# Seven products in place of eight for pairs of feature blocks in the first of two feed-forward stages

## The chip, the cores and the metric

One Trainium2 chip, one core of it. The metric is the device time in microseconds (us) of one execution of the whole program. The engines are TensorE (PE; the loads of its weights are shown as PEld), VectorE (DVE), ScalarE (ACT) and GpSimd (POOL); SyncE (SP) issues the loads.

## The reference

```python
def _moe_ref(x, w_gate, w_val, w_out):        # first stage, d_ff = 1536
    g = x @ w_gate
    silu = g * (1.0 / (1.0 + np.exp(-g)))
    val = x @ w_val
    return (silu * val @ w_out)

def _moe2_ref(x, w_in, w_out, alpha):         # second stage, d_ff = 2048
    h = x @ w_in
    g = np.maximum(h, 0.0) + alpha * np.minimum(h, 0.0)
    return (g @ w_out)

attn_out = _attn_ref(q, k, v, n_sink, window) # 2 batches, 8 heads, 768 positions, head size 64
x = attn_out.transpose(0, 2, 1, 3).reshape(1536, 512)
x = _moe_ref(x, w_gate, w_val, w_out)
return _moe2_ref(x, w_in, w_out, alpha)
```

The weights come as float64, 512 KB for 128 features. The result has the accuracy of float32.

## The kernel before

**The work.** 1536 tokens go through as three token blocks b = 0, 1, 2 of T = 512. Features are cut into blocks of 128: 12 in the first stage, 16 in the second. Every operand of a matmul is a pair of halves (h and l, type fp32r) whose sum is the float32 value, and a product of 128 rows of depth takes three matmuls of 512 columns: wh·xh, wh·xl and wl·xh. A block's projection (`proj`, L662) has four such rows of depth, so 12 matmuls.

**The weights.** `Stream` (L501) loads and converts them in the order of a list. SP loads a raw block (`raw`, three buffers); ACT takes its high words (Abs, L548, into `w_m`, two buffers); DVE puts the bits together (L584, L587, L590); ACT rounds to `wh` (L593); the rest `wl` is a subtraction (L599) on POOL if `idle_pool` is set, else on DVE. `step()` (L602) issues one stage of this after each piece of a unit. `idle_pool` is set during the attention and in the second stage. The `w_p` pool has 12 buffers for finished weights; chunk 1 of the first stage has 7 more (L1066).

**First stage.** `Moe1.unit(c, b)` (L688) takes a chunk c of four feature blocks and a token block b: gate projections `pg` (ACT makes `sg` with Silu, L710), value projections `pv` (DVE multiplies to `hid`, L718), the split of `hid` into `hh` (ACT, L679) and `hl` (DVE, L680), and four output products `po` of 12 matmuls each, which are copied (c = 0) or added by DVE (L742) to `acc`. 144 matmuls a unit, three chunks by three token blocks.

**Second stage.** `Duo.unit(c)` (L890) takes two feature blocks and all token blocks. Token blocks 0 and 1, the two feature blocks and the two halves of the depth form a 2 x 2 by 2 x 2 block product, which from c = 1 on is made with seven products of 6 matmuls (`product`, L835) and not eight. That needs sums of weights (kinds 2 and 3 in the list: POOL, L566 to L569, their `wh` by ACT, L572) and of tokens (`sums`, L819, 128x1024 operations taken one by one from the list `later`). Partial results stay in PSUM tiles `pa` and `pb`; ACT keeps copies of `pa` on the way (`keep`, L848, tiles p and u), which DVE adds to others (L855). Token block 2 goes through `proj`.

**Order.** The instructions' order on each engine is set by the framework's list scheduler from the order of the code; in the attention DVE's is as written. `verdict` (L362) makes a flag of range tests when the last weight is converted: one transpose `ps_flag` on PE, in the last but one unit of the second stage.

Of the kernel before, what the change touches and what calls it, by code (L numbers as in the profile page):

```python
# [35 lines left out]
WB = 12  # L36
WX = 7
RB = 3
VB = 6
# [20 lines left out]
def setup(nc, tc, ctx, g):  # L60
    const = ctx.enter_context(tc.tile_pool(name="const", bufs=1))
    g.const = const
    g.ident = const.tile([P, P], F32, name="ident")
    for nm in ("alpha", "sig", "sal", "sdn"):
        setattr(g, nm, const.tile([P, NF2], F32, name=nm))
    g.mask_a = const.tile([P, KW], F32, name="mask_a")
    g.mask_b = const.tile([P, KW], F32, name="mask_b")
    g.mask_0 = const.tile([P, P], F32, name="mask_0")
    g.mask_1 = const.tile([P, 2 * P], F32, name="mask_1")
    g.above = const.tile([P, P], I32, name="above")  # L70
    g.zero = const.tile([P, T], mybir.dt.bfloat16, name="zero")
# [83 lines left out]
def attention_pools(nc, tc, ctx, g):  # L155
    for nm, bufs in (("raw_p", VB), ("tr_p", TB), ("pr_p", 3), ("pt_p", 2), ("st_p", 4)):
        setattr(g, nm, ctx.enter_context(tc.tile_pool(name=nm, bufs=bufs)))
    g.nb = g.const.tile([P, B * H * NQ], F32, name="nb")
    g.wsum = g.const.tile([P, NW], F32, name="wsum")
    g.vsr = ctx.enter_context(tc.tile_pool(name="vs_p", bufs=1)).tile([P, NPAIR, NG * 2 * D], F32, name="vsr")  # L160
# [201 lines left out]
def verdict(nc, g):  # L362
    ok = g.const.tile([P, B * H * NQ], F32, name="ok")
    nc.vector.tensor_scalar(out=ok, in0=g.nb, scalar1=9.0e8, scalar2=None, op0=ALU.is_lt)
    red = g.red
    okw = g.const.tile([P, NW], F32, name="okw")
# [102 lines left out]
def weight_pools(nc, tc, ctx, g, sfx):  # L469
# [31 lines left out]
class Stream:  # L501
# [49 lines left out]
    def bits(self):  # L551
# [9 lines left out]
        if kind > 1:  # L561
# [10 lines left out]
            nc.scalar.activation(wh, m, AF.Copy)  # L572
# [5 lines left out]
        if slot is None or g.exact:  # L578
            nc.vector.tensor_scalar(out=m, in0=m, scalar1=WMAX, scalar2=-WMAX, op0=ALU.min, op1=ALU.max)
            w2 = g.w2_p.tile([P, KD * P], F32, tag="w2", name="w_2")  # L580
            sign, wi = mi, w2.bitcast(I32)
# [49 lines left out]
def moe1_seq(wg, wv, wo):  # L631
    seq = []
    for c in range(NF1 // CHUNK):
# [17 lines left out]
def duo_seq(wi, wo):  # L651

    seq = []
    for f in range(0, NF2, DUO):
        fs = range(f, f + DUO)
        seq += [(0, wi, x, DOWN, 3 * NF1 + x) for x in fs]
        seq += [(2, None, 0, None, None), (3, None, 0, None, None)] if f else []
        seq += [(1, wo, x, DOWN, 3 * NF1 + NF2 + x) for x in fs]
# [152 lines left out]
class Duo:  # L811
# [3 lines left out]
    def __init__(self, nc, g, st, base, ys, out, halves):  # L815
        self.nc, self.g, self.st, self.base, self.ys, self.out, self.halves = nc, g, st, base, ys, out, halves
        self.accs = {}

    def sums(self, a0, a1):  # L819

        nc, g = self.nc, self.g
        a, b, c, d = a0[:, 0:2], a0[:, 2:4], a1[:, 0:2], a1[:, 2:4]
        t1, t2, t4 = ([half(g.x_p2, n + z) for z in "hl"] for n in ("t1", "t2", "t4"))
        self.ts = ts = [t1, t2, [y[0] for y in self.ys[1]], t4]

        def sub(out, x, y):
            return lambda: nc.vector.tensor_tensor(out=out, in0=x, in1=y, op=ALU.subtract)

        def split(x, t):
            return lambda: split_hidden(nc, x, *t)  # L830

        self.last = split(c, ts[2])
        return [sub(a, c, a), sub(c, d, c), split(a, ts[0]), sub(d, d, a), split(d, ts[1]), sub(b, b, d), split(b, ts[3])]
# [19 lines left out]
    def add(self, ps, u):  # L853
        t = self.g.t_p.tile([P, T], F32, tag="hid", name="sum")
        self.nc.vector.tensor_tensor(out=t, in0=ps, in1=u, op=ALU.add)  # L855
        return t

    def bend(self, src, f, pair, inplace=False):
        nc, g = self.nc, self.g
        if inplace:  # L860
            hid = src
            nc.vector.scalar_tensor_tensor(
                out=hid, in0=src, scalar=g.alpha[:, f:f + 1], in1=src, op0=ALU.mult, op1=ALU.max
            )
        else:
            neg = g.t_p.tile([P, T], F32, tag="sg", name="neg")
            nc.scalar.activation(neg, src, AF.Copy, scale=g.alpha[:, f:f + 1])
            hid = g.t_p.tile([P, T], F32, tag="hid", name="hid2")
            nc.vector.tensor_tensor(out=hid, in0=src, in1=neg, op=ALU.max)
        split_hidden(nc, hid, *(t[:, f % 2] for t in pair))  # L870

    def plain(self):

        st, w, hids = self.st, self.base, {}
        for b, pool in ((0, None), (1, self.g.h_p2), (2, None)):
            hids[b] = hidden_pair(self.g, pool)
            for r in range(DUO):
                ph = self.new("ph")
                proj(self.nc, ph, st.get(w + r), *self.ys[b])
                self.bend(ph, r, hids[b])  # L880
                yield
            if b == 1:
                self.last()
        st.done(DUO)
        for b in range(3):
            for _ in self.outputs(0, b, w + DUO, *hids[b]):
                yield
        st.done(DUO)

    def unit(self, c):  # L890
        nc, g, st = self.nc, self.g, self.st
        if c == 0:
            yield from self.plain()
            return
        w = self.base + 2 * DUO + (c - 1) * 3 * DUO
        f = c * DUO
        (y0h, y0l), (y1h, y1l), y2 = self.ys
        b11, b21, b22 = (y0h[0], y0l[0]), (y0h[1], y0l[1]), (y1h[1], y1l[1])
        t1, t2, t3, t4 = self.ts
        hids = {0: hidden_pair(g)}  # L900
        pa, pb, pc = self.new("pa"), self.new("pb"), self.new("pc")
        self.product(pa, w, 0, b11, True)
        p1 = self.keep(pa, "p1")
        yield
        self.product(pc, w, 1, b21, True)
        self.bend(self.add(pc, p1), f, hids[0], True)
        yield
        self.product(pb, w + 2, 0, t1, True)
        yield
        self.product(pa, w + 2, 1, t2, False)  # L910
        u2 = self.keep(pa, "u2")
        yield
        hids[2] = hidden_pair(g)
        hids[1] = hidden_pair(g, g.h_p2)
        for r in range(DUO):
            ph = self.new("ph")
            proj(nc, ph, st.get(w + r), *y2)
            self.bend(ph, f + r, hids[2])
            yield
            if r == 0:  # L920
                self.product(pa, w + 3, 0, t3, False)
                u3 = self.keep(pa, "u3")
                self.bend(self.add(pb, u3), f + 1, hids[1], True)
                yield
        self.product(pa, w + 1, 1, t4, False)
        self.bend(pa, f + 1, hids[0])
        yield
        self.product(pb, w + 3, 1, b22, False)
        self.bend(self.add(pb, u2), f, hids[1], True)
        st.done(2 * DUO)  # L930
        yield
        for b in (2, 0, 1):
# [240 lines left out]
```

## Time and profile before

| | |
|---|---|
| three runs | 668.44, 670.21 (median), 671.40 us |
| the profiled execution, its own time | 670.04 us |
| its span, first to last instruction | 668.0 us |
| mean granted TensorE clock | 0.983 |
| busy: PE, DVE, ACT, POOL | 648.6, 430.7, 306.6, 158.6 us |
| first chunk's token block 2 starts | 181.09 us |
| 10 us windows with PE busy throughout at full clock | all from 180 to 660 us |

The span is what the trace shows; 2.0 us of the execution's own time lie outside it. PE is busy in 97% of the span, so what counts is how many matmuls there are, at which interval they follow each other, and where PE waits. Lines Lnnn are those of the kernel above. A matmul's own time (0.39 us) overlaps the next; the interval from one start to the next is what a matmul costs.

### The profile page before, as it was taken

The page shows a single profiled execution, that of the slowest core. Times are in us where ns is not written, and L with a number is a line of the kernel's source. Part 1 is how long each engine was busy: PE and PEld are TensorE (multiplying, and loading weights), DVE is VectorE, ACT ScalarE, POOL GpSimd, SP SyncE. Part 2 cuts the span into 40 slices and gives each one's busy share as a digit, 9 for nine tenths or more (in the row PEclk, how much of TensorE's full clock was granted, in tenths as well). Part 3 has the DMA queues.
Part 4 walks back from the last instruction along what each step waited for, and adds up shares of the span by engine and source line. Part 5 has one row for each costly group of instructions (what it writes and reads, how often), then busy time and mean ns, then how long its engine had stood idle before and what let it go on. Part 6 is the DMA issues. An engine that isn't in the chain of part 4 may idle for free.

```text
span 668.0 us, 8689 instructions
## 1 busy us (share of the span) xinstructions
PE 648.6 (97%) x3056; PEld 511.6 (77%) x3056; DVE 430.7 (64%) x915; ACT 306.6 (46%) x714; POOL 158.6 (24%) x203
## 2 busy tenths in 40 slices
PE   8879899999999999999999999999999999999996
PEld 4547566767788888888888888888888888888884
DVE  6897967355189852227432699938686969684654
ACT  4768755666366622024222356655344353533040
POOL 3547644334100000000000004614334251420000
PEclk8879899999999999999999999999999999999999
DMA  8754444100045620001300023222121303100005
GB/s 288 221 171 149 154 136 149 32 13 1 1 135 181 187 97 0 1 1 40 118 0 1 0 94 99 82 66 72 64 65 62 95 31 95 32 1 1 0 1 193
DMA packets 37203, 52.29 MB, mean 78 GB/s; under 512 B 4384, under 2 KB 28960, under 8 KB 37152
## 3 DMA queue, kind: packets, MB, share of 16 engines
q1 hardware_dynamic: 34944, 51.65, 24.2%
q8 instruction: 26, 0.43, 0.3%
q10 hardware_dynamic: 2208, 0.01, 0.2%
q14 instruction: 25, 0.20, 0.1%
HBM read 48.51 MB, written 3.15 MB: 77 GB/s over the span
## 4 chain that ended last, share of the span: by engine, by line
PE 88%; DVE 5%; ACT 3%; issue 1%; DMA 1%; POOL 1%; ACTq 0%; POOLq 0%
PE pf L947 7%; PE pf L948 7%; PE pf L949 7%; PE pa L841 6%; PE po L735 5%; PE pg L666 5%; PE po L736 5%; PE po L737 5%; PE pv L666 5%; PE pg L667 5%; PE pg L668 5%; PE pv L668 5%; PE pv L667 5%; PE pb L841 3%; PE ph L667 3%; PE ph L666 3%
## 5 line engine op out<-in xcount | busy, mean ns | idle before, releaser
L599 POOL TENSOR_TENSOR wl<-w_m,wh 128x512 fp32r<-128x512 f32 x44 | 57.9, 1322 | 99.1 <-ACT wh L593 87.1
L593 ACT ACTIVATE wh<-w_m 128x512 fp32r<-128x512 f32 x68 | 42.6, 629 | 76.9 <-PE pf L949 45.4
L947 PE MATMUL pf<-wh,hh 128*128 128x512 f32 x192 | 74.7, 389 | 0.0
L948 PE MATMUL pf<-wl,hh 128*128 128x512 f32 x192 | 74.7, 389 | 0.0
L679 ACT ACTIVATE hh<-hid 128x512 fp32r<-128x512 f32 x63 | 39.9, 633 | 66.7 <-DVE hid L718 51.7
L566 POOL TENSOR_TENSOR w_raw<-w_m 128x256 f32<-128x256 f32 x7 | 5.9, 840 | 253.0 <-DVE w_m L590 226.9
L949 PE MATMUL pf<-wh,hl 128*128 128x512 f32 x192 | 62.0, 389 | 0.0
L954 DVE TENSOR_TENSOR acc<-pf,acc 128x512 f32<-128x512 f32 x84 | 54.4, 681 | 11.4 <-PE pf L949 10.7
L718 DVE TENSOR_TENSOR hid<-pv,sg 128x512 f32<-128x512 f32 x36 | 24.7, 687 | 56.6 <-PE pv L668 56.5
L680 DVE TENSOR_TENSOR hl<-hid,hh 128x512 fp32r<-128x512 f32 x63 | 47.4, 754 | 20.7 <-ACT hh L679 20.3
L666 PE MATMUL pg<-xh,wh 128*128 128x512 f32 x144 | 57.5, 400 | 0.0
L666 PE MATMUL pv<-xh,wh 128*128 128x512 f32 x144 | 56.9, 395 | 0.0
L548 ACT ACTIVATE w_m<-w_raw 128x512 f32<-128x512 f32 x68 | 45.8, 674 | 24.0 <-DVE wl L599 9.6
L667 PE MATMUL pg<-xl,wh 128*128 128x512 f32 x144 | 56.7, 393 | 0.0
L668 PE MATMUL pg<-xh,wl 128*128 128x512 f32 x144 | 56.6, 393 | 0.0
L735 PE MATMUL po<-hh,wh 128*128 128x512 f32 x144 | 56.4, 395 | 0.0
L668 PE MATMUL pv<-xh,wl 128*128 128x512 f32 x144 | 56.1, 390 | 0.0
L667 PE MATMUL pv<-xl,wh 128*128 128x512 f32 x144 | 56.1, 389 | 0.0
L736 PE MATMUL po<-hh,wl 128*128 128x512 f32 x144 | 56.0, 390 | 0.0
L737 PE MATMUL po<-hl,wh 128*128 128x512 f32 x144 | 53.3, 390 | 0.0
L587 DVE SCALAR_TENSOR_TENSOR w_m<-w_raw,w_m 128x512 int32<-128x512 int32 x68 | 50.0, 736 | 1.1
L590 DVE SCALAR_TENSOR_TENSOR w_m<-w_raw,w_m 128x512 uint32<-128x512 uint32 x68 | 49.0, 723 | 0.6
(161 smaller groups left out, 1400.6 us busy)
## 6 DMA issues: line engine op xcount, KB each, us to landing
w_raw<-in_moe_w_out SPq DMA_DIRECT2D x28, 512.0 KB, 3.4
w_raw<-in_moe_w_in SPq DMA_DIRECT2D x16, 512.0 KB, 3.8
w_raw<-in_moe_w_gate SPq DMA_DIRECT2D x12, 512.0 KB, 4.4
w_raw<-in_moe_w_val SPq DMA_DIRECT2D x12, 512.0 KB, 4.4
th<-in_qk SPq DMA_DIRECT2D x16, 336.0 KB, 3.3
vr<-in_v SPq DMA_DIRECT2D x16, 192.0 KB, 2.6
out<-acc SPq DMA_DIRECT2D x12, 256.0 KB, 2.5
th<-in_qk SPq DMA_DIRECT2D x8, 256.0 KB, 5.1
```

The lines of the kernel that those rows point to most:

```text
L599: eng.tensor_tensor(out=wl, in0=m, in1=wh, op=ALU.subtract)
L666: nc.tensor.matmul(ps, wh[:, c], chan(xh, kk), start=(kk == 0), stop=False)
L667: nc.tensor.matmul(ps, wh[:, c], chan(xl, kk), start=False, stop=False)
L668: nc.tensor.matmul(ps, wl[:, c], chan(xh, kk), start=False, stop=(kk == KD - 1))
L735: nc.tensor.matmul(ps, wh[:, mc], hh, start=(x == 0), stop=False)
L736: nc.tensor.matmul(ps, wl[:, mc], hh, start=False, stop=False)
L737: nc.tensor.matmul(ps, wh[:, mc], hl, start=False, stop=(x == CHUNK - 1))
L841: self.nc.tensor.matmul(ps, a[:, c], m[:, k], start=(start and k == 0 and y == 0), stop=(k == 1 and y == 2), skip_group_check=True)
L947: nc.tensor.matmul(ps, hh[:, x, ts], wh, start=(x == 0), stop=False)
L948: nc.tensor.matmul(ps, hh[:, x, ts], wl, start=False, stop=False)
L949: nc.tensor.matmul(ps, hl[:, x, ts], wh, start=False, stop=(x == DUO - 1))
L954: nc.vector.tensor_tensor(out=av, in0=ps, in1=av, op=ALU.add)
```

## The change

Chunk 0 of the first stage stays. Its eight other feature blocks are taken by pairs by a new class `Duo1`: blocks 4, 5 plain; 6, 7 and 8, 9 with seven products for the gate and again for the value; 10, 11 plain, with the outputs. The code of the seven products becomes `Chain`, for both stages. The second stage keeps its steps.

```diff
-WB = 12
-WX = 7
+ORDER7 = (1, 2, 5, 6, 8, 7, 9, 4, 3)
+WB = 10
 RB = 3
+WA = 2
...
-            nc.scalar.activation(wh, m, AF.Copy)
+            nc.gpsimd.tensor_copy(wh, m)
             self.halves = (i, m, wh, wl)
...
+def duo1_seq(wg, wv, wo):
+
+    seq = []
+    for f in range(CHUNK, NF1, DUO):
+        fs = range(f, f + DUO)
+        more = SUMS if CHUNK < f < NF1 - DUO else []
+        seq += [(0, wg, x, DOWN, x) for x in fs] + more
+        seq += [(0, wv, x, DOWN, NF1 + x) for x in fs] + more
+        seq += [(1, wo, x, DOWN, 2 * NF1 + x) for x in fs]
+    return seq
...
+    def plus(self, ps, u, b, r):
+        t = self.room(b, r)
+        self.duo.nc.vector.tensor_tensor(out=t, in0=ps, in1=u, op=ALU.add)
+        self.sink(b, r, t, True)
+
+    def step(self, x):
+        d, w = self.duo, self.w
+        b11, b21, b22, t1, t2, t3, t4 = self.ops
+        if x == 1:
+            self.a = d.new("pa")
+            d.product(self.a, w, 0, b11, True)
+            self.p1 = d.keep(self.a, "u1")
+        elif x == 2:
+            ps = d.new("pc")
+            d.product(ps, w, 1, b21, True)
+            self.plus(ps, self.p1, 0, 0)
+        elif x == 6:
+            d.product(self.a, w + 2, 1, t2, False)
+            self.u2 = d.keep(self.a, "u2")
+        elif x == 5:
+            self.b = d.new("pb")
+            d.product(self.b, w + 2, 0, t1, True)
+        elif x == 7:
+            d.product(self.a, w + 3, 0, t3, False)
+            self.plus(self.b, d.keep(self.a, "u1"), 1, 1)
+        elif x == 4:
+            d.product(self.a, w + 1, 1, t4, False)
+            self.sink(0, 1, self.a, False)
+        elif x == 3:
+            d.product(self.b, w + 3, 1, b22, False)
+            self.plus(self.b, self.u2, 1, 0)
+        else:
+            ps = d.new("ph")
+            proj(d.nc, ps, d.st.get(w + x - 8), *self.more)
+            self.sink(2, x - 8, ps, False)
...
+        u, v = (g.h_p2.tile([P, 2, T], F32, tag=z, name="tsum") for z in ("hh", "hl"))
+        return [
+            self.sub(u, c[0], a[0]), self.add(u, u, c[1]), self.sub(u, u, a[1]),
+            self.sub(v, d[0], u), self.split(u, t1), self.add(v, v, d[1]),
+            self.sub(u, b[0], v), self.split(v, t2), self.add(u, u, b[1]),
+            self.sub(v, d[0], c[0]), self.split(u, t4), self.add(v, v, d[1]), self.sub(v, v, c[1]), lambda: self.third(v),
+        ]
...
+        def gate(b, r, src, own):
+            t = src if own else room_g(b, r)
+            nc.scalar.activation(t, src, AF.Silu)
+            gates[b, r] = t
...
+        def value(b, r, src, own):
+            hid = src if own else room_v(b, r)
+            nc.vector.tensor_tensor(out=hid, in0=src, in1=gates[b, r], op=ALU.mult)
+            split_hidden(nc, hid, *(t[:, r] for t in pairs[b]))
...
+        if c in (0, last):
+            yield from self.plain(w, c == last)
+            return
+        pairs = self.pairs()
+        room_g, gate, room_v, value = self.sinks(pairs)
+        for i, room, sink in ((0, room_g, gate), (2 * DUO, room_v, value)):
+            chain = self.chain(w + i, self.ops, self.xs[2], room, sink)
+            yield from chain.steps(ORDER7)
+            chain.done()
+        for b in (2, 0, 1):
+            for m in range(KD):
+                self.output(b, m, w + 4 * DUO, *pairs[b])
+                yield
+        self.st.done(DUO)
...
+        for x in range(DUO):
+            wh, wl = st.get(w + x)
+            nc.tensor.matmul(ps, wh[:, mc], hh[:, x], start=(x == 0), stop=False)
+            nc.tensor.matmul(ps, wl[:, mc], hh[:, x], start=False, stop=False)
+            nc.tensor.matmul(ps, wh[:, mc], hl[:, x], start=False, stop=(x == DUO - 1))
+        av = self.accs[b][0][:, m]
+        nc.vector.tensor_tensor(out=av, in0=ps, in1=av, op=ALU.add)
...
+    add_pool(nc, tc, early, g.w_ps, "w_pa", WA, "right")
+    st.own = range(3 * CHUNK)
...
+    for nm, bufs in (("x_p2", 6), ("u_p", 1), ("h_p2", 1), ("t_p2", 4)):
+        setattr(g, nm, ctx.enter_context(tc.tile_pool(name=nm, bufs=bufs)))
+    st.idle_pool = True
...
+    later.extend(d1.sums())
+    run([m1.unit(0, 2)])
+    assert g.w_ps.pop()[1] == WA
+    early.close()
+    last = (NF1 - CHUNK) // DUO - 1
     with ExitStack() as inner:
-        add_pool(nc, tc, inner, g.w_ps, "w_p2", WX)
-        run([m1.unit(0, 2)] + [m1.unit(1, b) for b in range(NPASS)])
-        assert g.w_ps.pop()[1] == WX
...
+        g.x_p3 = inner.enter_context(tc.tile_pool(name="x_p3", bufs=2, side="right"))
+        run([d1.unit(c) for c in range(last)])
+        assert not later
+    add_pool(nc, tc, ctx, g.w_ps, "w_p3", WA, "right")
+    st.own = range(base - 3 * DUO, len(st.seq))
+    run([d1.unit(last)] + [d2.unit(c, ys) for c in range(NF2 // DUO)])
```

The first change of code is that of the weight sums (kinds 2 and 3). Finished weights so have 12 buffers in chunk 0, 10 while the token sum t3 holds the place of two, and 12 from the last pair on. Masks and other constants of the attention move to a pool that ends with it, a temporary of the general path becomes the raw block's place, and `verdict` takes its scratch from the pool of `hid`.

The scheduler's order changes with it. PE, value products of blocks 8 and 9 (`pa`, `t2` to `t4` are the chain's partial result and token sums, `po` an output product of the same unit), as it is now:

```order
L1013 MATMUL po_3425<-hh_3082,wh_3097 128x512
L1014 MATMUL po_3425<-hh_3082,wl_3098 128x512
L846 MATMUL pa_3202<-t3h_2370,wh_3012 128x512
L846 MATMUL pa_3202<-t3l_2371,wh_3012 128x512
L846 MATMUL pa_3202<-t3h_2370,wl_3013 128x512
L846 MATMUL pa_3202<-t3h_2370,wh_3012 128x512
L846 MATMUL pa_3202<-t3l_2371,wh_3012 128x512
L846 MATMUL pa_3202<-t3h_2370,wl_3013 128x512
L1015 MATMUL po_3425<-hl_3083,wh_3097 128x512
L846 MATMUL pa_3202<-t4h_2049,wh_2979 128x512
```

Step 4 (t4) adds to `pa` one matmul after step 7 (t3), whose value ACT has to keep in between.

ACT, last pair of the first stage (blocks 10, 11), token block 2 (`w_m` are weights in conversion, `hh_3762` the upper half of the hidden pair that the outputs read, `yh` and `t1h`, `t2h` the second stage's tokens and token sums), as it is now:

```order
L953 ACTIVATE sg_3793<-ph_3780 128x512
L691 ACTIVATE yh_3713<-acc1_1899 128x512
L592 ACTIVATE wh_3847<-w_m_3826 128x512
L548 ACTIVATE w_m_3853,wsum_125<-w_raw_3573 128x512
L548 ACTIVATE w_m_3880,wsum_125<-w_raw_3599 128x512
L691 ACTIVATE hh_3762<-hid_3816 128x512
L691 ACTIVATE t2h_3758<-acc1_1899 128x1024
L691 ACTIVATE hh_3762<-hid_3841 128x512
```

The split of `hid_3816` stands behind a rounding and two steps of conversion; before, the outputs of a token block came from four hidden blocks and not from two.

PE, last but one unit of the second stage, before (`ps_flag` is the verdict's transpose, `pa`, `pb`, `pc` the chain's partial results, `t1` a token sum):

```order
L841 MATMUL pc_5376<-yl_3198,wh_4976 128x512
L841 MATMUL pc_5376<-yh_3196,wl_4977 128x512
L373 MATMUL ps_flag_5419<-ident_61,one_5417 1x128
L841 MATMUL pb_5375<-t1h_3463,wh_5012 128x512
L841 MATMUL pb_5375<-t1l_3464,wh_5012 128x512
```

and now:

```order
L846 MATMUL pa_5517<-t2l_3759,wh_5159 128x512
L846 MATMUL pa_5517<-t2h_3758,wl_5160 128x512
L846 MATMUL pa_5517<-yh_3712,wh_5175 128x512
L846 MATMUL pa_5517<-yl_3714,wh_5175 128x512
L846 MATMUL pa_5517<-yh_3712,wl_5176 128x512
L846 MATMUL pa_5517<-yh_3712,wh_5175 128x512
L846 MATMUL pa_5517<-yl_3714,wh_5175 128x512
L846 MATMUL pa_5517<-yh_3712,wl_5176 128x512
L373 MATMUL ps_flag_5560<-ident_61,one_5558 1x128
L846 MATMUL pb_5567<-t1h_3756,wh_5159 128x512
```

Steps 6 (t2) and 7 (y) now follow each other directly in `pa`, and the transpose and step 5 (t1) come behind them; before, step 5 stood ahead of step 6, and twelve matmuls of a projection lay between 6 and 7.

## Rows read from the trace of the kernel before

**Rows 1.** Page, part 1: busy time, share of the span, instructions.

```profile
PE 648.6 (97%) x3056; PEld 511.6 (77%) x3056; DVE 430.7 (64%) x915; ACT 306.6 (46%) x714; POOL 158.6 (24%) x203
```

**Rows 2.** Busy time by stretch; columns: stretch, then each engine, granted clock, DMA share, GB/s.

```profile
10.00:20.00 10.00, 8.83 (x43) 5.32 (x44) 8.51 (x36) 7.46 (x33) 5.01 (x6) 0.66 1.07 390
40.00:50.00 10.00, 8.70 (x41) 5.25 (x42) 8.81 (x44) 6.18 (x26) 4.37 (x6) 0.66 0.42 128
...
140.00:150.00 10.00, 9.16 (x54) 6.16 (x53) 5.01 (x21) 6.73 (x16) 2.21 (x5) 1.00 0.00 0
...
200.00:210.00 10.00, 10.00 (x45) 8.26 (x44) 9.74 (x19) 5.13 (x11) 0.00 (x0) 1.00 0.51 165
240.00:300.00 60.00, 60.00 (x267) 49.67 (x266) 14.62 (x23) 9.21 (x15) 0.00 (x0) 1.00 0.04 14
...
390.00:660.00 270.00, 270.00 (x1193) 223.50 (x1192) 198.42 (x313) 117.33 (x218) 75.82 (x66) 1.00 0.19 62
```

**Rows 3.** What PE waited for, whole span, largest and smallest: total, times, longest.

```profile
PE ps_s L224 <- ACT pr L234: 5.6, 8, 1.5
...
PE xp L320 <- POOL pt L295: 0.4, 1, 0.4
```

**Rows 4.** Timeline of PE, a pair of the second stage: start, length, instruction.

```profile
598.74 0.39 PE L841 MATMUL pa<-yh,wh 128*128 128x512 f32 x1
...
599.87 0.39 PE L841 MATMUL pa<-yh,wl 128*128 128x512 f32 x1
...
601.23 0.39 PE L841 MATMUL pc<-yh,wl 128*128 128x512 f32 x1
```

**Rows 5.** Timeline of ACT, the same place.

```profile
600.30 0.60 ACT L850 ACTIVATE p<-pa 128x512 f32<-128x512 f32 x1 [0.73 <-PE pa L841]
```

**Rows 6.** DVE by line and shape, 180 to 668: busy us, mean ns, idle before.

```profile
L599 DVE TENSOR_TENSOR wl<-w_m,wh 128x512 fp32r<-128x512 f32 x31 | 21.0, 685 | 2.1 <-ACT wh L593 1.9
L718 DVE TENSOR_TENSOR hid<-pv,sg 128x512 f32<-128x512 f32 x28 | 19.3, 688 | 49.5 <-PE pv L668 49.5
...
L742 DVE TENSOR_TENSOR acc<-po,acc 128x512 f32<-128x512 f32 x24 | 15.8, 686 | 24.1 <-PE po L737 23.8
...
L855 DVE TENSOR_TENSOR sum<-pb,u 128x512 f32<-128x512 f32 x14 | 9.6, 686 | 6.7 <-ACT u L850 6.7
...
L827 DVE TENSOR_TENSOR acc<-acc,acc 128x1024 f32<-128x1024 f32 x3 | 3.7, 1218 | 0.0
```

**Rows 7.** ACT by line and shape, 180 to 668.

```profile
L548 ACT ACTIVATE w_m<-w_raw 128x512 f32<-128x512 f32 x54 | 36.3, 673 | 21.4 <-DVE wl L599 9.6 <-POOL wl L599 6.1 <-POOL w_m L568 2.7
L593 ACT ACTIVATE wh<-w_m 128x512 fp32r<-128x512 f32 x56 | 35.0, 628 | 69.0 <-PE pf L949 45.4 <-PE pa L841 7.8 <-PE po L737 6.7
L679 ACT ACTIVATE hh<-hid 128x512 fp32r<-128x512 f32 x55 | 34.8, 632 | 60.3 <-DVE hid L718 45.3 <-DVE hid L869 15.0
...
L548 ACT ACTIVATION_READ_ACCUMULATOR w_m<-w_raw 128x1 f32 x54 | 10.3, 191 | 0.0
```

**Rows 8.** POOL by line and shape, 180 to 668.

```profile
L599 POOL TENSOR_TENSOR wl<-w_m,wh 128x512 fp32r<-128x512 f32 x32 | 42.6, 1339 | 77.0 <-ACT wh L593 64.9 <-PE pf L949 11.4
...
L568 POOL TENSOR_TENSOR w_m<-w_m 128x256 f32<-128x256 f32 x7 | 8.1, 1154 | 0.2
L567 POOL TENSOR_TENSOR w_raw<-w_raw,w_m 128x256 f32<-128x256 f32 x7 | 6.6, 938 | 0.1
L566 POOL TENSOR_TENSOR w_raw<-w_m 128x256 f32<-128x256 f32 x7 | 5.9, 840 | 253.0 <-DVE w_m L590 226.9 <-PE pa L841 26.1
L569 POOL TENSOR_TENSOR w_m<-w_m,w_raw 128x256 f32<-128x256 f32 x7 | 5.7, 808 | 0.0
```

**Rows 9.** Timeline of POOL, start of the second stage.

```profile
427.62 1.82 POOL L599 TENSOR_TENSOR wl<-w_raw,wh 128x512 fp32r<-128x512 f32 x1 [1.21 <-PE pf L949]
```

**Rows 10.** Timeline of DVE, the same place.

```profile
428.20 1.79 DVE L590 SCALAR_TENSOR_TENSOR w_m<-w_raw,w_m 128x512 uint32<-128x512 uint32 x1
```

More of the change, by code (lines that the diff above doesn't have):

```diff
@@ L628, in done, with moe1_seq @@
             self.n_done += 1
-def moe1_seq(wg, wv, wo):
+def moe1_seq(wg, wv, wo, chunks=NF1 // CHUNK):
     seq = []
-    for c in range(NF1 // CHUNK):
+    for c in range(chunks):
         fs = range(c * CHUNK, (c + 1) * CHUNK)
@@ L655, in duo_seq @@
         fs = range(f, f + DUO)
-        seq += [(0, wi, x, DOWN, 3 * NF1 + x) for x in fs]
-        seq += [(2, None, 0, None, None), (3, None, 0, None, None)] if f else []
+        seq += [(0, wi, x, DOWN, 3 * NF1 + x) for x in fs] + (SUMS if f else [])
         seq += [(1, wo, x, DOWN, 3 * NF1 + NF2 + x) for x in fs]
@@ L811, with __init__, sub, add @@
 class Duo:
[L815 to L833, printed above, removed]
+    def __init__(self, nc, g, st):
+        self.nc, self.g, self.st = nc, g, st
+    def sub(self, out, x, y):
+        return lambda: self.nc.vector.tensor_tensor(out=out, in0=x, in1=y, op=ALU.subtract)
+    def add(self, out, x, y):
+        return lambda: self.nc.vector.tensor_tensor(out=out, in0=x, in1=y, op=ALU.add)
+    def split(self, x, t):
+        return lambda: split_hidden(self.nc, x, *t)
     def product(self, ps, w, r, x, start):
@@ L872, in plain @@
[L872 to L932, printed above, removed]
-            for _ in self.outputs(c, b, w + 2 * DUO, *hids[b]):
-                yield
@@ new lines, in chain, with pairs, __init__, steps @@
+    def chain(self, w, ops, more, room, sink):
+        return Chain(self, w, ops, more, room, sink)
+    def pairs(self):
+        g = self.g
+        return {b: hidden_pair(g, pool) for b, pool in ((0, g.h_p), (2, g.h_p), (1, g.h_p2))}
+class Chain:
+    def __init__(self, duo, w, ops, more, room, sink):
+        self.duo, self.w, self.ops, self.more, self.room, self.sink = duo, w, ops, more, room, sink
+    def plus(self, ps, u, b, r):
[32 more added lines that the diff above has]
+            self.sink(2, x - 8, ps, False)
+    def steps(self, order):
+        for x in order:
+            self.step(x)
+            yield
+    def done(self):
+        self.duo.st.done(2 * DUO)
@@ L1063, in run @@
                     asked = True
-    with ExitStack() as inner:
-        add_pool(nc, tc, inner, g.w_ps, "w_p2", WX)
-        run([m1.unit(0, 2)] + [m1.unit(1, b) for b in range(NPASS)])
-        assert g.w_ps.pop()[1] == WX
-    for nm, bufs in (("x_p2", 6), ("u_p", 1), ("h_p2", 1)):
-        setattr(g, nm, ctx.enter_context(tc.tile_pool(name=nm, bufs=bufs)))
-    run([m1.unit(2, b) for b in range(NPASS)])
-    st.idle_pool = True
-    run([m2.unit(c) for c in range(NF2 // DUO)])
-    assert asked
+    later.extend(d1.sums())
+    run([m1.unit(0, 2)])
+    assert g.w_ps.pop()[1] == WA
+    early.close()
+    last = (NF1 - CHUNK) // DUO - 1
+    with ExitStack() as inner:
+        g.x_p3 = inner.enter_context(tc.tile_pool(name="x_p3", bufs=2, side="right"))
[4 more added lines that the diff above has]
+    run([d1.unit(last)] + [d2.unit(c, ys) for c in range(NF2 // DUO)])
+    assert asked and not later
 def general(nc, tc, g, q, k, v, w_gate, w_val, w_out, x2_in, x2_out, out):
```

171 lines of the change are left out of this document (132 added, 39 removed).

## The prediction

> **What bounds the kernel now.** I read the page first: PE is busy in 97% of the span, DVE in 64%, ACT in 46%, POOL in 24% [rows 1]. Then the busy time by stretch, because a share of the whole says nothing of a stage. From 390 to 660 us PE works for 270.00 of 270 us at full clock, and so it does in 240 to 300, where DVE has only 14.62 of 60 us of work [rows 2]. PE's waits come next: the list for the whole span begins with 5.6 us and ends with 0.4, and all of it is of the attention (ps_s, xp, ps_p) [rows 3]; from 170 us on it is empty. So behind the attention the time is the number of matmuls times their interval. The timeline of PE gives that interval: from 598.74 to 601.23 eleven of them, 0.2264 us each [rows 4]. The 0.39 us of a row is a matmul's own length and overlaps the next. A matmul taken out there is worth 0.226 us, one waited for costs the wait, and work on another engine costs nothing as long as PE finds its operands in time.
>
> **What is removed from PE.** A seven-product chain has 42 matmuls for token blocks 0 and 1 where eight products have 48. The change makes four such chains: gate and value, for blocks 6, 7 and for 8, 9. That is 4 x 6 = 24 matmuls, and 24 x 0.2264 = 5.43 us. The other matmuls (token block 2, outputs, both plain pairs) are as many as before. The attention keeps its order on PE up to the first chunk, and the second stage has the same steps, so I cost both at nothing, but for one place below.
>
> **What is added on the other engines, and why most of it costs nothing.** The outputs of a pair of blocks are six matmuls long and not twelve, so 48 additions come where DVE had 24 at 686 ns (L742): 16.5 us more. Twelve additions of kept partial results at 686 ns (L855) are 8.2 us. The token sums are ten operations and four splits of 128x1024 at 1218 ns (L827): 17.1 us. Off DVE go the `wl` subtractions, 31 at 685 ns: 21.2 us [rows 6]. Net 20.6 us on an engine that has 237 us free [rows 1]. By stretch the tightest is the first chunk's token block 2 with the sums, where DVE had 9.74 of 10 us already [rows 2], part of it those subtractions. I put it at up to 38 us of work in a unit of 33, but its late pieces (the sums) are needed only a unit later, and the plain pair between (216 matmuls, 49 us) takes up the rest. A seven-product unit has about 34 us of DVE work in 204 matmuls or 46 us. POOL gets 40 subtractions at 1339 ns, four weight sums of 840 + 938 + 1154 + 808 = 3740 ns [rows 8] and the 22 roundings of sums that ACT did or would do. A rounding on POOL is not in the trace; I bound it by ACT's 628 ns [rows 7] and POOL's 1339 for a subtraction, and take the latter, being POOL's own row of the same size: 29 us. Sum 98 us, on an engine that was idle from 180 to 390 us. The four extra weight pairs need no loads. The loads on SP's queue are as many as before; with 12 or 10 buffers in place of 19 they start later, but a weight is still finished 15 us or more before PE's order asks for it, by my count of the matmuls between. Constants that moved cost nothing for the same reason: they are in place when their readers start, as before.
>
> **Where PE now has to wait.** What a short chain costs is read at the second stage, where the same steps run. The last matmul of a `pa` product starts at 599.87 [rows 4], ACT begins to copy it at 600.30 and takes 0.60 [rows 5]. A matmul that writes to `pa` again can follow 0.43 + 0.60 = 1.03 us after that start, which is four and a half intervals. In three places of the new order the distance is smaller than the chain:
> 1. Blocks 8, 9, value: step 4 follows step 7 with one output matmul between, two intervals. 1.03 - 0.45 = 0.58 us. Nothing shortens it; it is longer, up to 1.4, if ACT is in a conversion step (673 + 191 ns [rows 7]) just then. I take 0.6.
> 2. Last pair, token block 2: `hh_3762` stands on ACT behind the rounding `wh_3847`, which waits for the weight buffer that PE gives back 14 matmuls ahead of the reader `po_3861`, and behind a conversion step that waits for POOL's subtraction from that rounding (two `w_m` buffers). Chain: 0.43 + 0.63 (rounding) + 1.34 (POOL [rows 8]) + 0.67 + 0.19 (conversion) + 0.63 (`hh`) [rows 7] = 3.89 us against 14 x 0.2264 = 3.17. I take 0.7; the bounds are 0 (the rounding finds its buffer earlier) and 1.4 (DVE is in a 1218 ns sum as `hid_3816` comes).
> 3. Last but one unit of the second stage: steps 6 and 7 are neighbours. 1.03 - 0.23 = 0.80 us; there were twelve matmuls between.
> 4. First plain pair, token block 0: `hh_2327` is behind the conversion of `w_m_2429`, which waits for the weight sums on POOL (two subtractions and L566 to L568, 2 x 1.34 + 2.93 = 5.6 us). By my count of what lies between it just fits or misses by 0.5; if POOL is late by half of that chain, 3 us. I take 0.3, near the end that the count gives.
>
> Everywhere else I find a margin: the least is 0.6 us, at the first split of the first seven-product unit, and the others are 1.2 or more.
>
> Rows that stretch two of these terms: a POOL subtraction beside a DVE operation took 1.82 us, and DVE's 1.79 where its mean row is 0.72 [rows 9, 10]. The Trainium skill ("GPSIMD Engine Reference", section 1, Specifications) says that POOL shares its SBUF interfaces with VectorE and that they contend when DVE has two SBUF inputs; these two rows agree, and by that rule place 2 would use 1.82 and not 1.34, which makes its term 1.2 and the sum 667.5. I stay with the mean over 32 of them, which has such meetings in it.
>
> **The sum.** The profiled execution took 670.04 us, 668.0 of it span; it is 0.17 below the median of the three runs, which is nothing beside their own spread of 3 us. 670.04 - 5.43 + 0.6 + 0.7 + 0.8 + 0.3 = **667.0 us**. Smallest terms (0.58, 0, 0.80, 0): 666.0. Largest (1.4, 1.4, 0.8, 3): 671.2. What a measurement of this kernel can tell from no change is about 0.5%, 3.4 us: below 666.86 is faster, above 673.56 slower. The forecast sits at that line: a real gain of which half is given back.
>
> **The rivals.**
> - *No wait remains.* The order is a list; engines run ahead where they can, and if the kept copies and splits come a little sooner than in my chains, all of 5.43 us stays: 664.6. For it: the second stage runs the same chain seven times with no wait of PE [rows 2]. Against it: places 1 and 3 are closer than any place there, and a copy of 0.60 us cannot be hidden behind one matmul.
> - *POOL holds up everything (slower).* With `wl`, the sums and their roundings on POOL and only two `w_m` buffers, the conversion step after each of the four new sum pairs waits for two subtractions and the sum, 2.68 + 3.74 = 6.4 us, and it stands on ACT and DVE ahead of the copies and splits that PE needs next. If the cover is the twelve matmuls of one projection (2.7 us), PE loses 3.7 us at each: 664.6 + 4 x 3.7 = 679.4. From 2.2 us each on it is slower by over 0.5% (8.9 us in all). For it: ACT's conversion steps already wait for POOL (6.1 and 2.7 us of their idle time [rows 7]), and meetings with DVE stretch POOL further [rows 9]. Against it: the same sum pairs in the second stage cost PE nothing in 270 us [rows 2], with the same two buffers.
> - *A wait takes the clock down.* In 10 to 20 and 40 to 50 us PE was busy for 8.83 and 8.70 of 10 us and the granted clock was 0.66; with 9.16 it stayed at 1.00 [rows 2]. The waits that I count leave 9.2 or more. If one of them is as long as there (1.2 us), the 10 us are worth 6.6: one such fall costs 3.4 us, and the time is 667.0 + 3.4 = 670.4, no change.
> - *DVE becomes the bound in the first chunk's last unit.* If PE does have to wait for DVE's 38 us in 33, 5 us: 672.0. It needs a sum ahead of a split that PE reads soon; in the order the sums stand behind them or a unit ahead.
>
> **How the numbers follow.** The forecast has 0.58, no wait at all 0.20, a fall of the clock or DVE as the bound together 0.10, POOL 0.12. Faster by over 0.5%: the second case, and nearly half of the first (666.0 to 666.86, where the unknown terms are at their low ends): 0.47. Slower: POOL's, 0.12. The rest, 0.41, lies within 0.5%. The range goes from 664.5 (no wait) to 671.0, which takes in the largest terms and the fall of the clock and leaves out POOL's case and half of DVE's. The likeliest case's own range is 666.0 to 669.
>
> **What the profile of the changed kernel would show.** PE: 24 matmuls fewer, interval 0.226, and a list of PE's waits behind 170 us that is no longer empty: three or four entries of 0.3 to 1 us, `pa` after the kept copies (L855) in two places and `po` after `hh`. If the list is empty, the first rival holds; if it has entries of 2 us and more for `hh` or `wl` behind POOL, the second. The granted clock should be 1.00 in every stretch from 180 us on. DVE should show about 450 us, POOL about 255. The forecast is wrong if the attention ends at another time than 181.09, for which I have no term, or if a fifth place appears.

## The result and the profile after

The changed kernel takes 674.14 us (median of six runs, 673.59 to 675.3) against 669.38 before; the ratio is 1.0069, interval 1.0052 to 1.0086. It is slower by 0.7%; I had forecast 667.0, and 664.5 to 671.0 as the range. The profiled execution took 675.3 us, its span is 673.6.

The page and the list of PE's waits from 170 us on, of the changed kernel (engine, line, waited for; total, times, longest):

```profile
PE 650.3 (97%) x3032; PEld 508.5 (75%) x3032; DVE 473.9 (70%) x933; ACT 308.5 (46%) x716; POOL 245.2 (36%) x281
```

```profile
PE po L1013 <- ACT hh L691: 4.5, 2, 2.5
PE pa L846 <- ACT u L855: 1.1, 2, 0.7
```

PE has the 24 matmuls fewer [rows 1]. The list, empty before, has two lines of two waits each, and these are the four places that I had named. DVE is busy for 473.9 us where I had forecast about 450, POOL for 245.2 and not 255. The waits as listed start where the last matmul's 0.39 us end; what a wait costs is the interval from start to start less the usual 0.2265. Worked out so from the starts of all matmuls, between the attention's last matmul and the last of all (the stretch, 480.14 us before and 484.12 now):

| term | forecast | measured, us |
|---|---|---|
| 24 matmuls fewer | -5.43 | -5.44 |
| place 1, step 4 behind step 7 | 0.6 | 0.62 |
| place 2, last pair, token block 2 | 0.7 | 2.70 |
| place 3, step 7 behind step 6 | 0.8 | 0.85 |
| place 4, first plain pair, token block 0 | 0.3 | 2.14 |
| first interval behind a wait, and one more of that size, 5 x 0.11 | none | 0.55 |
| matmuls that follow each other more slowly | none | 2.55 |
| sum | -3.0 | +3.97 |

The sum is the measured +3.98. In this execution the attention ends 2.02 us later too, one of the signs that the prediction named for its being wrong; 1.2 us of it come where the granted clock stays low for longer, 0.73 in 80 to 90 us against 0.88 before. The change does not make it so each time: two executions of the same order of instructions below (e2, e10) had their attention as short as before, 179.74 and 179.73 us from the first matmul against 179.81. So what there is to explain is two waits, and matmuls that got slower without any wait.

**Place 4.** POOL, ACT, DVE and PE of the changed kernel in the first plain pair (start, length, instruction; in brackets the idle time before):

```profile
220.94 1.83 POOL L598 TENSOR_TENSOR wl<-w_m,wh 128x512 fp32r<-128x512 f32 x1 [2.85 <-ACT wh L592]
222.72 0.75 POOL L566 TENSOR_TENSOR w_raw<-w_m 128x256 f32<-128x256 f32 x1
223.42 1.30 POOL L598 TENSOR_TENSOR wl<-w_m,wh 128x512 fp32r<-128x512 f32 x1
224.67 0.75 POOL L567 TENSOR_TENSOR w_raw<-w_raw,w_m 128x256 f32<-128x256 f32 x1
225.50 0.74 POOL L568 TENSOR_TENSOR w_m<-w_m 128x256 f32<-128x256 f32 x1
```

```profile
226.27 0.66 ACT L548 ACTIVATE w_m<-w_raw 128x512 f32<-128x512 f32 x1 [3.02 <-POOL w_m L568]
226.83 0.19 ACT L548 ACTIVATION_READ_ACCUMULATOR w_m<-w_raw 128x1 f32 x1
228.40 0.63 ACT L691 ACTIVATE hh<-hid 128x512 fp32r<-128x512 f32 x1 [1.38 <-DVE hid L961]
```

```profile
227.05 0.72 DVE L583 TENSOR_SCALAR w_m<-w_m 128x512 int32<-128x512 int32 x1 [5.44 <-ACT w_m L548]
227.69 0.68 DVE L961 TENSOR_TENSOR hid<-ph,sg 128x512 f32<-128x512 f32 x1
```

```profile
226.72 0.39 PE L680 MATMUL ph<-xh,wl 128*128 128x512 f32 x1
229.08 0.50 PE L1013 MATMUL po<-hh,wh 128*128 128x512 f32 x1 [1.98 <-ACT hh L691]
```

This is the chain that I had written down, POOL's sums and then the conversion step on ACT, with one link more: that step's first half on DVE, and only then `hid` and `hh`. DVE is idle for 5.44 us, though the last matmul of the product that `hid` reads had started 12 intervals ahead of 226.72; `hid` stood second in DVE's queue.

**Place 2.** DVE, POOL and ACT in the last pair of the first stage, changed kernel:

```profile
399.20 2.60 DVE L692 TENSOR_TENSOR yl<-acc,yh 128x512 fp32r<-128x512 f32 x2
401.72 1.21 DVE L692 TENSOR_TENSOR t1l<-acc,t1h 128x1024 fp32r<-128x1024 f32 x1
402.86 2.31 DVE L832 TENSOR_TENSOR acc<-acc 128x1024 f32<-128x1024 f32 x1
405.10 0.68 DVE L692 TENSOR_TENSOR yl<-acc,yh 128x512 fp32r<-128x512 f32 x1
405.70 0.68 DVE L961 TENSOR_TENSOR hid<-ph,sg 128x512 f32<-128x512 f32 x1
```

```profile
399.64 1.61 POOL L598 TENSOR_TENSOR wl<-w_m,wh 128x512 fp32r<-128x512 f32 x1
402.35 1.73 POOL L598 TENSOR_TENSOR wl<-w_m,wh 128x512 fp32r<-128x512 f32 x1 [1.10 <-ACT wh L592]
```

```profile
404.12 0.67 ACT L548 ACTIVATE w_m<-w_raw 128x512 f32<-128x512 f32 x1 [1.19 <-POOL wl L598]
...
406.41 0.63 ACT L691 ACTIVATE hh<-hid 128x512 fp32r<-128x512 f32 x1 [1.52 <-DVE hid L961]
```

PE at the same place, the last matmul of the product that this `hid` reads and the first one that waits for `hh`:

```profile
401.44 0.39 PE L680 MATMUL ph<-xh,wl 128*128 128x512 f32 x1
...
407.09 0.50 PE L1013 MATMUL po<-hh,wh 128*128 128x512 f32 x1 [2.54 <-ACT hh L691]
```

The matmuls between the two, up to 404.16, make the other block's product. My chain over POOL ends on ACT at 404.9; by itself it would have cost about 1.2 us (an estimate: `hh` from 404.9 with its 0.63, against PE's next turn at 404.39). But `hh` starts 1.5 us later, because `hid` is late. Its product is there from 401.8 on, and DVE first works off splits and token sums for almost 4 us: one of 128x1024 beside POOL's subtraction takes 2.31, the one ahead of it 1.21.

**The slow matmuls.** PE in the second stage of the changed kernel; the moving operand is a weight in one of the two lent buffers at the upper end of the memory:

```profile
441.60 0.40 PE L1098 MATMUL pf<-wh,hh 128*128 128x512 f32 x1
...
443.00 0.40 PE L1098 MATMUL pf<-wh,hh 128*128 128x512 f32 x1
```

Six intervals in 1.40 us, 0.2333 each, with no wait between. By the program's addresses it is the 312 matmuls whose moving operand lies in those two buffers (t3 first, then weights): 6.6 ns longer than 0.2265 on the mean, the others 0.4. In the kernel before, where all operands start at the same offset within 256 bytes, the mean is 0.2 ns over 0.2265. What such small differences come to, without waits and the intervals behind them, I call the small excess: 2.96 us here, 0.40 before. Nothing in my prediction had a term for that.

### The profile page after: what moved, and what is told of

It reads as the page before. It is cut to its first block, busy times and chain, and to the rows that moved or that the text cites. A ratio compares the mean times of both kernels' runs of the same rounds, so it can differ in the third digit from the quotient of the medians.

```text
span 673.6 us, 8796 instructions
## 1 busy us (share of the span) xinstructions
PE 650.3 (97%) x3032; PEld 508.5 (75%) x3032; DVE 473.9 (70%) x933; ACT 308.5 (46%) x716; POOL 245.2 (36%) x281
## 4 chain that ended last, share of the span: by engine, by line
PE 84%; DVE 7%; ACT 4%; POOL 2%; issue 1%; DMA 1%; SPq 0%; POOLq 0%; ACTq 0%
PE pa L846 9%; PE pf L1100 7%; PE pf L1099 7%; PE pf L1098 7%; PE ph L678 6%; PE ph L679 6%; PE ph L680 6%; PE pb L846 4%; PE po L1013 3%; PE po L1014 3%; PE po L1015 3%; PE ps_s L224 2%; PE xp L320 2%; PE pc L846 2%; PE po L747 2%; PE po L748 2%
## 5 line engine op out<-in xcount | busy, mean ns | idle before, releaser
L598 POOL TENSOR_TENSOR wl<-w_m,wh 128x512 fp32r<-128x512 f32 x79 | 111.6, 1419 | 197.8 <-ACT wh L592 172.9
L583 DVE TENSOR_SCALAR w_m<-w_m 128x512 int32<-128x512 int32 x68 | 34.5, 508 | 38.6 <-ACT w_m L548 38.6
L680 PE MATMUL ph<-xh,wl 128*128 128x512 f32 x128 | 49.8, 389 | 0.0
L679 PE MATMUL ph<-xl,wh 128*128 128x512 f32 x128 | 49.8, 389 | 0.0
L678 PE MATMUL ph<-xh,wh 128*128 128x512 f32 x128 | 49.8, 389 | 0.0
L234 ACT ACTIVATE pr<-ps_s,nb 128x160 f32<-128x160 f32 (+2 forms) x96 | 38.0, 406 | 19.0 <-DVE nb L230 16.4
L224 PE MATMUL ps_s<-th 64*128 64x288 f32 (+2 forms) x192 | 41.1, 461 | 5.8 <-ACT pr L234 4.8
L1100 PEld LDWEIGHTS pf<-wh,hl 128*128 128x128 f32 x192 | 36.0, 188 | 8.1
L1098 PEld LDWEIGHTS pf<-wh,hh 128*128 128x128 f32 x192 | 36.0, 188 | 8.1
L1099 PEld LDWEIGHTS pf<-wl,hh 128*128 128x128 f32 x192 | 36.0, 188 | 8.1
```

The lines of the kernel that those rows point to most:

```text
L224: nc.tensor.matmul(pss[e][:, :first + w], self.th[r, qs], self.th[r, ks], start=True, stop=True)
L598: eng.tensor_tensor(out=wl, in0=m, in1=wh, op=ALU.subtract)
L678: nc.tensor.matmul(ps, wh[:, c], chan(xh, kk), start=(kk == 0), stop=False)
L679: nc.tensor.matmul(ps, wh[:, c], chan(xl, kk), start=False, stop=False)
L680: nc.tensor.matmul(ps, wl[:, c], chan(xh, kk), start=False, stop=(kk == KD - 1))
L1098: nc.tensor.matmul(ps, hh[:, x, ts], wh, start=(x == 0), stop=False)
```

## The experiments

All times stand beside runs of the kernel before on the same chip: one execution of 668.89 us for e1 to e4, medians of 669.99 for e5 to e7 and of 669.75 for e8 to e10. e6, e8 and e9 were run several times, the others once; there I compare the stretch, and name a fall of the clock in it.

### e1 and e2: does the place slow the matmuls?

```diff
+    pad_p = ctx.enter_context(tc.tile_pool(name="pad_p", bufs=1, side="right"))
+    pad_p.tile([P, 56], F32, name="pad")
     early = ExitStack()
```

> The changed kernel with 224 unused bytes ahead of the two buffers at the upper end of the memory, so that t3 and the lent weight buffers start 224 bytes lower (at a multiple of 256 bytes, not 224 past one); nothing else moves. In the changed kernel the stretch from the attention's last matmul to the last start of a matmul is 484.13 us, and 312 matmuls whose moving operand lies there follow each other at 0.2331 us on the mean and not 0.2269. Theory A, it is the start address within 256 bytes: their mean interval falls to 0.227, the stretch to 482.2. Rival B, it is the upper end of the memory itself: both stay within 0.3 us. The four waits of PE stay as they are in both.

```diff
+    const.tile([P, 32], F32, name="pad_l")
     g.ident = const.tile([P, P], F32, name="ident")
```

> The changed kernel with 128 unused bytes ahead of all tiles at the lower end: every other tile now starts 224 bytes past a multiple of 256, as t3 and the lent weight buffers do and did. Theory A (start address within 256 bytes): about 1700 more matmuls get an interval longer by 6 ns, so the stretch grows from 484.1 to about 494 us. Rival B (place at the upper end): 484.1 within 0.3 us.

Both theories fell. e1: 675.48 us, stretch 486.14 with one fall of the clock; the 312 matmuls stay slow (7.6 ns). e2: 670.99 us, stretch 481.89; they are fast (0.2 ns) although they did not move, and no other became slow (0.3 ns). So neither the upper end nor its own offset makes an operand slow. What e2 changed is that both sides start at the same offset.

### e5 and e10: equal offsets

```diff
+    pad_p.tile([P, 32], F32, name="pad")
```

> The changed kernel with 128 unused bytes ahead of the buffers at the upper end, so that those start 96 bytes past a multiple of 256 as all other tiles of this kernel do. In the left shift both sides started 224 past and the slow intervals were gone (27 left of 217), in the right shift by 224 they stood at 0 and 96 and were slow; so what counts would be the two operands' starts against each other. Theory G (equal offsets within 256 bytes are fast, unequal ones slow): the 312 matmuls' mean interval falls from 0.2331 to 0.227, the small excess in all from 3.0 us to under 1, the stretch to 482.2 (if the clock does not fall behind a wait; 1.5 us more for each time it does). Rival H (224 past is good and 96 is bad for the lower end's tiles): the interval stays at 0.233.

> The changed kernel with 384 unused bytes ahead of the buffers at the upper end: 256 more than in e5, so that the two sides agree within 256 bytes but not within 512 or 2048. If equality within 256 bytes is what counts, the 312 matmuls stay at 0.2267 us and the small excess under 1 us. If it is within 512 or more, up to a tile's 2048, they are slow again, 0.232 to 0.234, and the excess is about 3 us. The order is the changed kernel's, with its four waits.

The pad stands where e1 has its own. e5: 673.56 us, the 312 matmuls at 0.2 ns, small excess 0.65 us in all (2.96 in the changed kernel); its stretch is 483.52, since the clock fell once behind a wait. e10 is e5 with 96 numbers in the pad: again 0.2 ns, stretch 481.91, 670.99 us. PE in e10, the place shown above:

```profile
438.94 0.39 PE L1098 MATMUL pf<-wh,hh 128*128 128x512 f32 x1
...
440.30 0.39 PE L1098 MATMUL pf<-wh,hh 128*128 128x512 f32 x1
```

Six intervals in 1.36 us. Offsets (within 256 bytes) of 0 and 0, 224 and 224, 96 and 96 are fast, 96 and 224 and 96 and 0 slow; e10's sides differ by 256 and are fast. Theory G holds, at 2.3 us for this kernel. The changed kernel also has the pair the other way round, in 24 matmuls from 183.1 us on: there the stationary operand lies in a lent buffer and the moving one elsewhere, and their intervals behind the first are 6.6 ns longer on the mean too (6.5 in e1). So it is the two operands of one matmul that have to agree.

### e3 and e4: what stands ahead of the splits

```diff
+def behind(tc, key, f):
+    if key in LAST and LAST['on']:
+        with tc.issue_after(LAST[key]):
+            f()
+    else:
+        f()
...
-                    later.pop(0)()
+                    behind(tc, "hid", lambda: behind(tc, "hh", later.pop(0)))
```

> The changed kernel with the token sums of both stages held behind the last product with the gates (hid) on DVE and behind its split on ACT, from the first plain pair on. The wait of PE in the last pair of the first stage (token block 2, po for hh) is 2.70 us over the usual interval. Theory C, DVE had a backlog of token sums and splits ahead of hid, stretched by POOL's subtractions beside them: the wait falls under 0.4 us, the stretch from 484.1 to about 481.7. Rival D, what I predicted for this place (rounding, POOL's subtraction and the conversion step ahead of the split on ACT): 1 us or more of it stays, the stretch is 482.5 or more.

```diff
-            self.bits()
+            behind(self.tc, "hid", self.bits)
...
-            self.start()
+            behind(self.tc, "hh", self.start)
```

> The changed kernel with conversion steps in the first plain pair issued behind the last split (on ACT) and the last product with a gate (on DVE), in the code's order, not ahead of them; POOL's work is the same. The wait of PE there (token block 0, po for hh) is 2.14 us over the usual interval. Theory E, the conversion step that waits for POOL's weight sum stands ahead of the split and holds it up: the wait goes, and nothing takes its place; the stretch falls from 484.1 to 482.0. Rival F, POOL is too slow for the weights of this unit and what is held up moves on: a wait of 1 us or more appears later, for a weight half or a split, and the stretch stays above 483.

e3 has this from the first plain pair to the last, e4 its own edit in the first plain pair alone. e4: 673.92 us. Place 4's wait is gone, and up to place 1 no interval is more than 0.11 us over the usual one: theory E. The stretch shows little of it (484.01), because the clock fell behind place 2's wait. Busy time by stretch in e4, columns: stretch, its length, PE, PEld, DVE, ACT and POOL with counts, granted clock, DMA share, GB/s:

```profile
398.00:404.00 6.00, 3.58 (x16) 2.63 (x14) 6.00 (x7) 2.62 (x6) 2.03 (x2) 1.00 0.00 0
404.00:408.00 4.00, 3.88 (x12) 3.10 (x13) 4.00 (x6) 1.65 (x3) 0.00 (x0) 0.67 0.00 0
408.00:412.00 4.00, 4.00 (x18) 3.25 (x17) 4.00 (x7) 2.27 (x3) 0.10 (x1) 0.90 0.12 16
```

PE had waited 2.5 us; after it resumed, eight matmuls follow each other at 0.427 us, the lower of the two levels (1.2 GHz), 1.6 us in all. e1, e3 and e5 show one such fall each, at place 2 or 4; the changed kernel's own profile and e2, e7, e10 show none at the same waits.

e3: 675.73 us, stretch 485.85 with one fall of the clock, behind place 4's wait. Place 2's wait shrinks by 1.07 us to 1.63 and not under 0.4, so theory C is half right: what left DVE's queue ahead of `hid` is the split `t1l` (1.21 us); a token sum of 1.21 is still there. What is left is not theory D's chain, though. DVE, POOL in e3:

```profile
399.53 2.60 DVE L706 TENSOR_TENSOR yl<-acc,yh 128x512 fp32r<-128x512 f32 x2
402.05 1.21 DVE L846 TENSOR_TENSOR acc<-acc 128x1024 f32<-128x1024 f32 x1
403.19 1.78 DVE L706 TENSOR_TENSOR yl<-acc,yh 128x512 fp32r<-128x512 f32 x1
404.89 0.68 DVE L975 TENSOR_TENSOR hid<-ph,sg 128x512 f32<-128x512 f32 x1
```

```profile
399.97 1.61 POOL L599 TENSOR_TENSOR wl<-w_m,wh 128x512 fp32r<-128x512 f32 x1
402.68 1.74 POOL L599 TENSOR_TENSOR wl<-w_m,wh 128x512 fp32r<-128x512 f32 x1 [1.10 <-ACT wh L593]
```

ACT waits for `hid` again, and `hid` for the sum and for a split that took 1.78 us beside POOL and takes 0.68 alone. A new wait of 1.08 us came up in the second stage, for the lower half `hl` of a split that DVE made late.

### e7: POOL's subtractions taken away

```diff
-    st.idle_pool = True
+    st.idle_pool = False
     asked = False
...
-    run([d1.unit(last)] + [d2.unit(c, ys) for c in range(NF2 // DUO)])
+    run([d1.unit(last)])
+    st.idle_pool = True
+    run([d2.unit(c, ys) for c in range(NF2 // DUO)])
```

> The changed kernel with the first stage's low weight halves subtracted on DVE as before the change, not on POOL; POOL keeps the weight sums and their roundings. If POOL's subtractions stretch DVE's work (theory C's second half), single operations of DVE beside them of 1.6 to 2.3 us disappear between 183 and 400 us; in the first plain pair the wait of 2.14 us shrinks under 0.5, since POOL has nothing ahead of the sums. In exchange DVE has some 20 us more to do: if DVE's load alone decides, waits of 1 to 3 us appear in the second pair with seven products and stay in the last pair, and the stretch is 485 or more; if not, it falls to 481.

671.86 us, stretch 482.43. DVE's operations with two inputs over 1.4 us between 183 and 400 us: 12 in the changed kernel, none here. DVE by line, 183 to 420 us, changed kernel and e7:

```profile
L692 DVE TENSOR_TENSOR hl<-hid,hh 128x512 fp32r<-128x512 f32 x29 | 24.7, 857 | 6.7 <-ACT hh L691 6.6
```

```profile
L598 DVE TENSOR_TENSOR wl<-w_m,wh 128x512 fp32r<-128x512 f32 x37 | 25.4, 692 | 12.6 <-ACT wh L592 11.0 <-PE ph L680 1.6
...
L692 DVE TENSOR_TENSOR hl<-hid,hh 128x512 fp32r<-128x512 f32 x30 | 20.7, 696 | 5.0 <-ACT hh L691 4.9
```

Between 183 and 400 us DVE is busy for 164.7 us and not 155.8, so 27 us of subtractions cost it 9 net; the rest it gets back. The Trainium skill ("GPSIMD Engine Reference", section 1, Specifications) names a cause, SBUF interfaces shared by the two engines, with contention when DVE has two SBUF inputs; that they are what slows it is the page's word, that it ends when POOL's work goes is this run's. Place 4's wait is gone, place 2's is still 1.97: DVE's queue ahead of `hid` is long without POOL too. A wait of 1.07 appears in the second pair with seven products, as the load theory wanted; both count.

### e6, e8 and e9: all repairs together, and the seven products without them

e6 has e2's shift, e3's and e4's order through all pairs of the first stage, and the verdict one piece later, which takes place 3 away; e8 is e6 with e7's edit; e9 is e6 with plain pairs only and without sums (`FLAG` is 1):

```diff
                 if not asked and st.n_conv == len(st.seq):
-                    verdict(nc, g)
                     asked = True
+                    late = FLAG
+                elif late:
+                    late -= 1
+                    if not late:
+                        verdict(nc, g)
```

```diff
-    st.idle_pool = True
+    st.idle_pool = False
```

```diff
-        more = SUMS if CHUNK < f < NF1 - DUO else []
+        more = []
...
-        if c in (0, last):
+        if True:
             yield from self.plain(w, c == last)
             return
```

> The changed kernel with the left shift by 128 bytes, with conversion steps and token sums issued behind the last split and product with a gate from the first plain pair to the last, and with the verdict one piece of a unit later. If theories C and E and the shift account for the time: waits of PE of 2.14, 0.62, 2.70 and 0.85 us shrink to 1.5 us in all, the small excess to under 1, the stretch to 476.5 to 478 against 480.14 before the change, and the time is 666 to 667, 0.4 to 0.5% faster than before. If the waits are POOL's doing (rival F), they appear elsewhere and the stretch stays above 480, the time at 670 or more.

> e6 (left shift, work issued in the code's order, verdict later) with the first stage's low weight halves on DVE as in e7. In e6 the 12 operations of DVE over 1.4 us between 183 and 400 us are still there, and waits of 1.04 and 0.47 us with them. If POOL's subtractions beside DVE are what is left of the waits (theory C's second half), those two fall under 0.3 us each; the wait of 0.86 us between steps 7 and 4 of the second pair stays as in e7, since its chain has no POOL in it; stretch 476.2 to 476.8 and time 665.5 to 666.3. If DVE's load decides, a wait of over 1 us appears and the stretch is 478 or more.

> e6 with blocks 6 to 9 as plain pairs too: no seven products, no token or weight sums in the first stage, 24 matmuls more; the order rules, the shift and everything else as in e6. If the 24 matmuls are worth what the interval says and their sums cost PE nothing, the stretch grows from 477.1 by 5.4 less the 1.8 us of waits that the sums may be behind, so 480.7 to 482.5, and the time is 670 to 672. If the sums cost as much as the products save, the stretch is 477 to 479.

| | time, us | ratio to before | interval | stretch | waits of PE |
|---|---|---|---|---|---|
| e6 | 666.37 | 0.9950 | 0.9934 to 0.9967 | 477.07 | 1.04, 0.47, 0.17 |
| e8 | 665.43 | 0.9938 | 0.9925 to 0.9951 | 475.91 | 0.85 |
| e9 | 673.18 | 1.0050 | 1.0038 to 1.0062 | 484.05 | three of 0.93, 0.53 |

PE's waits from 170 us on in e8, then in e9:

```profile
PE pa L862 <- ACT u L871: 0.7, 1, 0.7
```

```profile
PE po L1030 <- ACT hh L705: 2.7, 4, 0.8
```

e6 and e8 beat both kernels; e6 came out close to its numbers (1.68 us of waits, forecast 1.5), e8 0.3 us of stretch under them: with POOL's subtractions off, only the wait that no queue causes (step 4 behind step 7) is left. e9 loses 7.0 us of stretch to e6, more than expected: 5.4 are the matmuls; 1.6 are waits, not behind sums but in plain pairs, at the first outputs. ACT in e9, at the first of its three waits of 0.93:

```profile
274.04 0.67 ACT L551 ACTIVATE w_m<-w_raw 128x512 f32<-128x512 f32 x1 [0.52 <-POOL wl L601]
274.62 0.18 ACT L551 ACTIVATION_READ_ACCUMULATOR w_m<-w_raw 128x1 f32 x1
274.71 0.61 ACT L705 ACTIVATE hh<-hid 128x512 fp32r<-128x512 f32 x1
```

`hid` had ended at 273.45; `hh` stands behind a conversion step that had waited for POOL's subtraction, and so it does at the two others. Plain pairs with POOL's subtractions lose 3.9 us to chunks of four (484.05 against 480.14), which the seven products have to earn back first; how much of that pairs cost without those subtractions was not run.

## Why the prediction was wrong

- The gain (-5.43) and places 1 and 3 (0.6 and 0.8) were right in mechanism and size: 5.44, 0.62, 0.85. They rest on one chain read in rows 4 and 5.
- Place 4 was right in mechanism; the size was the wrong choice. The bounds were 0 and 3; I took 0.3, from a count with mean rows, and it was 2.14. POOL's part of the chain was not longer than charged: its first subtraction took 1.83 and not 1.34, but the sums less than their mean rows, and all of it ran from 220.94 to 226.24, 5.3 us and not 5.6. What I had not charged is that DVE's half of the conversion (0.72) also stands ahead of `hid`. The rest of the miss, 1.4 us, lies in my count of what stands between, which the prediction does not write out.
- Place 2 was wrong in mechanism, and this is the step that failed. I followed the ACT queue over POOL (0.7) and took DVE into account with one sum of 1.2 us at most (the bound of 1.4); DVE's queue ended last, with two operations of 128x1024 and a split ahead of `hid` and one of them stretched by POOL, and the wait was 2.70. My second figure for this place, 1.2 with POOL's 1.82, charged POOL's side only; it is about what the chain over POOL would have cost, but the larger cost was on DVE, where a meeting adds up to 1.1 us to an operation.
- "A margin everywhere else" held: no fifth wait appeared. But a matmul's interval was not the constant that the prediction took from eleven intervals at one place: most of the 2.55 us came from two buffers at another offset than the rest (2.3 of them go in e5). No row of before could show it, since there all operands share one offset. The 0.55 us of longer intervals behind waits had no term either.
- The rival with a wait that takes the clock down: its mechanism is real (four of the experiments), at 1.6 us a fall and not 3.4, and it comes and goes at the same wait. The rows that it was built on did not carry it: 20 to 30 and 70 to 80 us of the kernel before show PE busy for less, 7.56 and 7.69 of 10 us, at a higher clock, 0.89 and 0.95. How much of the median it carries stays open.
- The rival that ends slower, POOL in front of everything, was half of the truth: the time did end in its part of the forecast. But there were two large waits, of 2.1 and 2.7 us, and not four of 3.7. The first is POOL's through a queue, and goes with its subtractions (e7). Of the second only a part is POOL's, through DVE's speed: without POOL's subtractions 1.97 us were left (e7), with a shorter queue ahead of `hid` 1.63 (e3), and with both nothing (e8).

The sum with the measured terms, 667.0 + 1.84 (place 4) + 2.0 (place 2) + 0.55 + 2.55 = 673.9, comes near the median of 674.14. That is in part luck: it starts from the profiled execution of before, 670.04, and from the median of the six, 669.38, the same terms give 673.3. The other 0.8 us are in no term; longer attentions or falls of the clock in some of the runs would be enough, which only a trace of each could show.

## What to carry to other kernels

When work moves to an idle engine, look at what it does to the engine beside it and at who stands behind its results in an in-order queue. Here POOL had 78.1 us of work between 183 and 400 us, and 24.2 when its subtractions went back to DVE; having them on POOL cost the stretch 1.7 us in the changed kernel (against e7) and 1.2 with the work in order (e6 against e8). A scheduler that issues whatever is ready first can put a conversion step ahead of a split that PE needs at once, though PE first read that step's weight 53 us later: pinning it in the code's order took away the wait of 2.1 us (e4). And a matmul's interval is worth checking against the addresses: make separately allocated pools start at the same offset within 256 bytes.

## What the runs showed of the hardware that I had not expected

Matmuls of 512 columns followed each other at 0.2331 us on the mean, not 0.2267, where the starts of moving and stationary operand differed by 128 bytes within 256 (changed kernel), and at 0.2341 where they stood at 0 and 96 (e1); a difference of 0 or 256 was fast (e2, e5, e10). Why it is so stays open. The first interval after a listed wait was 0.11 us longer (0.333 to 0.341 and not 0.2265) in every run, wherever the clock did not fall with it. In e1, e3, e4 and e5 the clock fell once behind a wait of 2.2 to 2.7 us; behind waits as long it did not fall in the changed kernel's own profile, in e2 and in e10.
